# The head of an adaLN block: keys and values by partial sums, modulation rows spread by transfers, a new order of work

## The chip, the cores and the metric

One core of one Trainium2 chip. The metric is the device time of one launch in microseconds (us), here the median of several runs of the same kernel. Engines: PE is TensorE, PEld its weight loads, DVE is VectorE, ACT is ScalarE, POOL is GpSimd, SP is the engine whose queue issues most transfers.

## The reference, cut to what matters

A transformer block with adaptive layer norm: 2048 rows of 512, 32 query heads of 16 that share one head of keys and values, and a dense layer of 1792 with relu.

```python
mod = (_silu(c) @ w_mod).reshape(c.shape[0], 6, 1, -1)
sa, ca, ga, sb, cb, gb = (mod[:, 0], mod[:, 1], mod[:, 2], mod[:, 3], mod[:, 4], mod[:, 5])
h = _layernorm(x, axis=-1) * (1 + ca) + sa
x = x + ga * _A_ref(h, A_wq, A_wk, A_wv, A_wo)     # attention: softmax(q k / sqrt(16)) v, then wo
h = _layernorm(x, axis=-1) * (1 + cb) + sb
x = x + gb * _B_ref(h, B_w1, B_w2)                 # relu(h w1) w2
```

## The kernel before, in words

All engines run an order written out by hand; each engine takes its instructions in that order. The kernel has three stages.

**The head** (up to the first matmul on the values, L1053). The 2048 rows come in four blocks b of 512. A block is loaded (`load_x`), its row sums are taken, it is normalised in place, turned (`tr1`, a transposition of 128 columns at a time through a `ps_exp` bank, then ScalarE writes `hT` with the modulation as scale and bias), and then keys and values (`kv`) and the first six of 16 query projections (`qproj_now`, one at a time in the bank `ps_fill`) are made from it. The first unit of queries needs the maxima of its scores before its exponentials can run: `max_of` makes 48x512 scores in one of four banks (three `ps_max`, one `ps_more`) and VectorE takes their maximum. There are 64 such steps for unit 0, 16 for each 512 keys (`kb`), in the order of `kb`, and 16 for unit 1.

The string `FIRST` is the order of the head after block 0 is turned. Each letter emits one step on all engines that it needs:

- `A`, `B`: the two halves of the first query projection; each ends with a low part on VectorE (L410), which frees its `ps_exp` bank
- `x`, `y`: row statistics of 128 rows of block 1, block 2, on VectorE (L233); `s`: the same for block 3, on ScalarE (L302, L304); `c`, `E`, `f`: the ends of these statistics for blocks 1, 2, 3 (`E` and `f` mostly on GpSimd, begun by three small VectorE instructions); `c`, `r`, `g`: the rows of blocks 1, 2, 3 are normalised, two on GpSimd (L326), two on ScalarE (L329)
- `t`: one transposition step; `q`: a quarter of a query projection (four matmul instructions of 256 columns); after four of them ScalarE copies the bank out and rounds it (L278, L266) and GpSimd makes the low part
- `k`: one step of `kv`; `m`: one maximum; `d`: one block of scores and its exponential; `o`: one step of the modulation rows; `w`: a dummy matmul; `L`, `l`: loads of queries and weights on SP

`kv` before: four matmuls of 128 rows and 512 columns add up in one bank, ScalarE copies values and keys out (L374, L377: keys as rounded `fp32r`), then the rest that rounding left (the low part, 16 rows of `kp` in each half of the partitions) is made on GpSimd (L385), for block 0 on VectorE (L383). The maxima over these keys need the low parts: half 1 first, then half 0. Last step: the values are turned and VectorE copies them out (L391).

`mod_all` before: 16 narrow matmuls (32 output rows, four side by side in the array) give four partial rows for one modulation vector, and a matmul with `firsts` adds them up and spreads them over 128 partitions (L216). It runs for four vectors: two gates (`gr`), `sbr` and `cbr`. The rows for the first layer norm are made earlier by `mod_row` and `mod_col`.

A query tile's row maxima go through DRAM: `max_rows` transposes them, ScalarE and GpSimd split them, SP stores them and loads them back as two rows of the query tile (L494, L500). Only then can `d` run for that unit.

**The main loop**: 256 cycles `c`. A cycle has eight score blocks with exponentials, eight maxima for a later unit, eight narrow matmuls on the values, and a portion of the dense layers or query projections, in halves of 64 rows. Strings such as `PARTS` give the order in a cycle, and `hook` the position in it at which put-off work is emitted (`put_off`: roundings of tiles that a portion has finished).

**The last cycles** (`ending`, from the point where no maxima are left) have 20 positions (`LAST`, `APART`), all before the values. In some of them the put-off work is the relu and rounding of the hidden layer on ScalarE, then VectorE (L733, L734). After that comes the last block alone.

Of the kernel before, what the change touches and what calls it, by code (L numbers as in the profile page):

```python
# [35 lines left out]
FIRST = ("AxxxkkkxykLwqcykyqyqBEmmmmttqkttsrmmmmkklkmmmsmqqstmmmmq"  # L36
         "qstmmmmkfqqtmmmmkktmmgmmkkmmmmtqtqtmmmmkkkmmmmtkmmkmmomm"
         "mmqqmmmmkommommmqmmmommmommqmmmqoqommmmoqdmmdddmmdmqmmdd"
         "md")
# [25 lines left out]
def build(tc, nc, cst, sb, ps, dr, x, wq, wk, wv, wo, w1, w2, c, w_mod, out):  # L65
# [18 lines left out]
    def chunks(ap):  # L84
        return ap.rearrange("(k p) n -> p k n", p=P)
# [31 lines left out]
    wkv0 = sb.tile([P, DC, 2, DH], F32, name="wkv0", tag="stg", bufs=3)  # L117
    nc.sync.dma_start(wkv0[:, :, 0], chunks(wk))
    nc.sync.dma_start(wkv0[:, :, 1], chunks(wv))
    load_x(1)  # L120
    load_wq(1)
# [20 lines left out]
    firsts = cst.tile([P, P], F32, name="firsts")  # L142
    nc.gpsimd.memset(firsts, 0.0)
    for k in range(DC):
        nc.gpsimd.memset(firsts[k * 32:k * 32 + 1], 1.0)
    wkv = sb.tile([P, 512], F32, name="wkv", tag="pvs", bufs=1)
    wkvr = wkv.rearrange("p (k a n) -> p k a n", k=DC, a=8)
# [63 lines left out]
    def mod_all(i, dst, bank):  # L211

        row = mod_row(i, ps_exp())
        yield
        pt = bank()
        nc.tensor.matmul(pt, firsts, row, start=True, stop=True)  # L216
        nc.scalar.activation(dst, pt, AF.Copy, bias=1.0 if i == 4 else 0.0)
        yield
# [143 lines left out]

    def kv(b):

        bs = slice(b * LB, (b + 1) * LB)
        pt = ps_exp()
        for k in range(DC):
            nc.tensor.matmul(pt, wkv[:, k * P:(k + 1) * P], hT[b][:, k],  # L368
                             start=k == 0, stop=k == DC - 1)
            if k < DC - 1:  # L370
                yield
        vT = sb.tile([P, LB], F32, name="vT", tag="tmp", bufs=2)
        if b:
            nc.scalar.activation(vT, pt, AF.Copy)  # L374
        for g in (1, 0):
            r = slice(g * 64, g * 64 + 48)
            nc.scalar.activation(kp[r, bs], pt[r], AF.Copy)  # L377
        if b == 0:
            nc.scalar.activation(vT, pt, AF.Copy)
        for g in (1, 0):  # L380
            r = slice(g * 64 + 32, g * 64 + 48)
            if b == 0:
                nc.vector.tensor_tensor(kp[r, bs], pt[r], kp[r, bs].bitcast(F32), op=OP.subtract)  # L383
            else:
                nc.gpsimd.tensor_tensor(kp[r, bs], vT[r], kp[r, bs].bitcast(F32), op=OP.subtract)  # L385
        yield
        pv = ps_exp()
        for t in range(4):
            nc.tensor.transpose(pv[:, t * 32:(t + 1) * 32], vT[32:64, t * P:(t + 1) * P],
                                idn[32:64, 32:64])  # L390
        nc.vector.tensor_copy(  # L391
            vt[:, b * 4:(b + 1) * 4, 0:DH],
            pv[:, 0:128].rearrange("p (t n) -> p t n", n=32)[:, :, 16:32])
        yield
# [571 lines left out]
    def sums_of(b):  # L966
        for t in range(4):
# [8 lines left out]
                          wqs.rearrange("p k (a d) -> p k d a", d=DH))  # L976
    for j in range(8):
        nc.gpsimd.tensor_copy(wkvr[:, :, j], wkv0[:, :, 1 if j % 4 == 3 else 0])
# [8 lines left out]
    mods = [mod_all(i, dst, ps_exp) for i, dst in  # L987
            ((2, gr[:, 0]), (5, gr[:, 1]), (3, sbr), (4, cbr))]
# [4 lines left out]
                 o=itertools.chain(*mods))  # L993
    early = [(s, ct) for cts in ((1, 3), (0, 2)) for s in range(2) for ct in cts]
    waiting, ready = list(first_max), 0
    for what in FIRST:
        if what == "m":
            assert waiting[0][4] < (ready + 1) // (DC + 1)
# [11 lines left out]
        elif what == "l":  # L1010
            load_q(1)
        elif what == "d":
# [48 lines left out]
    for c in range(NU * KT // 2):  # L1061
# [19 lines left out]
        hook = 9 if parts is QUERIES else 3  # L1081
# [77 lines left out]
```

## Time and profile before

| | |
|---|---|
| median of 3 runs | 1604.93 us (1603.21 to 1607.35) |
| profiled execution | 1607.23 us, of which the span of the engines' work is 1605.3 us |
| busy in the span | PE 99%, PEld 56%, DVE 85%, ACT 75%, POOL 24% |
| granted TensorE clock | 0.999 |
| head | up to 95.2 us |

The profile lists busy time of each engine, groups of instructions by line with their mean duration and the idle time of the engine before them (with what ended it), the chain of work that ended last, and timelines. Times in a row of the timeline are start and duration in us; a bracket at the end gives the idle time before it and the instruction that ended it.

### The profile page before, as it was taken

How to read it: one execution, taken by the hardware profiler on the slowest of the kernel's cores; microseconds unless marked ns; L12 is line 12 of the kernel's file. 1: busy time of each engine (PE TensorE's matmuls, PEld its weight loads, DVE VectorE, ACT ScalarE, POOL GpSimd, SP SyncE). 2: the span in 40 equal slices, each digit the busy share in tenths (PEclk: the TensorE clock that was granted, in tenths of full speed). 3: DMA queues.
4: the chain of work that ended last, by engine and by line, in shares of the span. 5: the costliest groups of instructions: out<-in, count | busy, mean ns of one | idle time of the engine just before them, and what ended most of it. 6: DMA issues, size and time to landing. Idle time of an engine off the chain costs nothing.

```text
span 1605.3 us, 33595 instructions
## 1 busy us (share of the span) xinstructions
PE 1591.2 (99%) x12919; PEld 900.3 (56%) x12919; DVE 1358.4 (85%) x2377; ACT 1207.2 (75%) x2368; POOL 379.6 (24%) x581
## 2 busy tenths in 40 slices
PE   8999999999999999999999999999999999999999
PEld 5545454446655565556655565556655565546668
DVE  6889999998889888998889988898889988898331
ACT  4567888778877887778877787778877788778931
POOL 3323365541113110141112211131112311131010
PEclk9999999999999999999999999999999999999999
DMA  8334543323211330114201331113201331122331
GB/s 268 121 111 132 163 128 94 104 85 99 69 37 51 99 106 17 61 44 128 70 24 48 98 106 32 51 55 116 83 20 47 89 109 42 37 69 93 128 131 54
DMA packets 96486, 137.16 MB, mean 85 GB/s; under 512 B 24328, under 2 KB 59852, under 8 KB 96328
## 3 DMA queue, kind: packets, MB, share of 16 engines
q1 hardware_dynamic: 96048, 134.83, 27.1%
q8 instruction: 103, 1.69, 0.4%
q14 instruction: 55, 0.45, 0.1%
q10 hardware_dynamic: 280, 0.20, 0.0%
HBM read 104.00 MB, written 28.82 MB: 83 GB/s over the span
## 4 chain that ended last, share of the span: by engine, by line
PE 94%; DVE 3%; ACT 1%; DMA 1%; issue 0%; POOL 0%; POOLq 0%; SPq 0%; PEldq 0%; DVEq 0%; ACTq 0%
PE ps_pv L1053 31%; PE ps_exp L909 22%; PE ps_fill L185 19%; PE ps_max L530 16%; DVE pm L532 1%; PE ps_exp L162 1%; PE ps_max L162 1%; PE ps_fill L162 1%; PE ps_exp L368 1%; ACT pe L911 1%; DMA xb<-in_A_x_dram 0%; DMA recs<-rc 0%; PE ps_max L172 0%; PE ps_max L909 0%; PE ps_exp L335 0%
## 5 line engine op out<-in xcount | busy, mean ns | idle before, releaser
L532 DVE TENSOR_REDUCE pm<-ps_max 128x1 f32<-128x512 f32 x2022 | 1258.4, 681 | 142.0 <-PE ps_max L530 122.0
L911 ACT ACTIVATE pe<-ps_exp 128x512 f32<-128x512 f32 x2017 | 1062.9, 605 | 285.0 <-PE ps_fill L185 124.5
L530 PE MATMUL ps_max<-kp,qp 48*128 48x512 f32 x2022 | 836.8, 425 | 0.7 <-DVE pm L532 0.7
L909 PE MATMUL ps_exp<-qp,kp 50*128 50x512 f32 x2017 | 752.6, 414 | 2.3 <-ACT pe L911 2.1
L1053 PE MATMUL ps_pv<-pe,vt 128*32 128x512 f32 x4096 | 543.8, 604 | 0.0
L909 PEld LDWEIGHTS ps_exp<-qp,kp 50*128 50x128 f32 x2017 | 352.0, 185 | 300.7 <-ACT pe L911 182.2
L530 PEld LDWEIGHTS ps_max<-kp,qp 48*128 48x128 f32 x2022 | 369.0, 185 | 211.0 <-DVE pm L532 179.8
L185 PE MATMUL ps_fill<-w2r,r 64*128 64x512 f32 x1008 | 273.2, 403 | 0.0
L185 PE MATMUL ps_fill<-hh,w1s 64*128 64x256 f32 x1472 | 214.5, 286 | 0.1
L185 PEld LDWEIGHTS ps_fill<-hh,w1s 64*128 64x128 f32 x1472 | 193.2, 187 | 0.5 <-PEq L178 0.4
L185 PEld LDWEIGHTS ps_fill<-w2r,r 64*128 64x128 f32 x1008 | 175.1, 184 | 8.0
L1053 PEld LDWEIGHTS ps_pv<-pe,vt 128*32 128x32 f32 x4096 | 82.0, 108 | 129.5 <-issue 111.8
L267 POOL TENSOR_TENSOR r<-stg,r 128x512 fp32r<-128x512 f32 x46 | 59.2, 1286 | 276.0 <-ACT r L266 269.1
L185 PE MATMUL ps_fill<-hl,w1s 64*128 64x256 f32 x736 | 118.3, 280 | 0.0
L185 PEld LDWEIGHTS ps_fill<-hl,w1s 64*128 64x128 f32 x736 | 99.5, 186 | 0.0
L185 PE MATMUL ps_fill<-hT,wq 64*128 64x256 f32 x320 | 81.9, 375 | 0.0
L1116 POOL TENSOR_TENSOR on<-num,den 128x256 f32<-128x256 f32 x31 | 22.8, 737 | 238.6 <-DMA den<-recs 144.8
L185 PEld LDWEIGHTS ps_fill<-hT,wq 64*128 64x128 f32 x320 | 59.4, 186 | 5.5
L925 POOL COPY num<-pvs 128x256 f32<-128x256 f32 x32 | 12.7, 398 | 196.0 <-ACT pvs L921 196.0
L491 POOL TENSOR_TENSOR ms<-sq,ms 128x32 fp32r<-128x32 f32 x28 | 7.1, 255 | 138.8 <-ACT ms L486 138.8
L278 ACT ACTIVATE stg<-ps_fill 128x512 f32<-128x512 f32 x61 | 37.5, 614 | 0.5 <-PE ps_fill L162 0.5
L185 PE MATMUL ps_fill<-wol,oh 64*128 64x512 f32 x112 | 36.6, 407 | 0.0
(194 smaller groups left out, 1020.7 us busy)
## 6 DMA issues: line engine op xcount, KB each, us to landing
w1s<-w1dr SPq DMA_DIRECT2D x104, 512.0 KB
qp<-qdr SPq DMA_DIRECT2D x64, 192.0 KB
qdr<-qq SPq DMA_DIRECT2D x39, 256.0 KB
raw<-in_B_w_dram SPq DMA_DIRECT2D x28, 256.0 KB
w1dr<-w1s SPq DMA_DIRECT2D x14, 512.0 KB
wmod<-in_w_mod_dram SPq DMA_DIRECT2D x6, 1024.0 KB
x<-in_A_x_dram SPq DMA_DIRECT2D x8, 512.0 KB
out_dram<-ot SPq DMA_DIRECT2D x16, 256.0 KB
```

The costliest lines, as they stand in the source:

```text
L162: nc.tensor.matmul(pt[0] if isinstance(pt, tuple) else pt, w, a, start=start, stop=stop is True)
L185: ins = nc.tensor.matmul(pt, w[r], a[r], start=start and h == 1, stop=stop and h == 0)
L267: (eng or nc.gpsimd).tensor_tensor(lo, src, hi.bitcast(F32), op=OP.subtract)
L278: nc.scalar.activation(stg, pt, func, **kw)
L368: nc.tensor.matmul(pt, wkv[:, k * P:(k + 1) * P], hT[b][:, k], start=k == 0, stop=k == DC - 1)
L530: nc.tensor.matmul(pt, qps[u][i][r, j * P:(j + 1) * P], kp[r, kb * 512:(kb + 1) * 512], start=True, stop=True)
L532: nc.vector.tensor_reduce(pms[u][:, (hf * 2 + i) * 4 + j, kb:kb + 1], pt, axis=AX.X, op=OP.max)
L909: nc.tensor.matmul(pt, kp[r, kt * P:(kt + 1) * P], qps[u][ct // 2][r], start=True, stop=True)
L911: nc.scalar.activation(pe, pt, AF.Exp)
L925: nc.gpsimd.tensor_copy(num, pvs[:, 0:TB])
L1053: nc.tensor.matmul(pvt[at:at + 32], vt[:, kt], pes.pop((s, i)), start=(kt == 0), stop=(kt == KT - 1))
L1116: due[1]()
```

## The change

Keys and values: the four matmuls of a block get 32 output rows each and run side by side in four column groups, so a bank holds four partial sums of 32 rows. ScalarE copies it to a tile (`each`), and one matmul with `gather` (ones in the right places, made on GpSimd from the identity) adds the four and spreads keys and values over the partitions as before. `kv` has three steps in place of five. The weights are loaded straight into place. The first keys' low parts go to GpSimd and get a letter of their own, `p`.

Modulation rows: one routine `mods_all` does all four vectors in two steps `o`. Vector n has the column group n, and the four parts of its sum add up in the bank. ScalarE copies the bank out (twice, one with bias 1.0); the rows are stored to DRAM and loaded back to 128 partitions by broadcasting loads on SP.

Order: a new string `FIRST`, without `w`; the load of the second part of `wq` moves ahead of block 1. In the last cycles `hook` is 19 in place of 3: a portion's roundings are emitted behind the scores of the cycle that finished it, not among the scores of the next.

```diff
-FIRST = ("AxxxkkkxykLwqcykyqyqBEmmmmttqkttsrmmmmkklkmmmsmqqstmmmmq"
-         "qstmmmmkfqqtmmmmkktmmgmmkkmmmmtqtqtmmmmkkkmmmmtkmmkmmomm"
-         "mmqqmmmmkommommmqmmmommommqmmmqoqommmmoqdmmdddmmdmqmmdd"
-         "md")
+FIRST = ("xxAxxkqkLcpyyyyEBkqttttmmmmkmmmmksmmmmqkrsmmmmqslmmmmtts"
+         "fmmmmttmmmmkmmmmkqgkmmmmttmmmmttmmmmkqmmmmkqkmmmmqqmmmmq"
+         "qmmmmqqmmmmqqqommmqommmmqqdmmdddmmdqmmddmmd")
...
-    wkv0 = sb.tile([P, DC, 2, DH], F32, name="wkv0", tag="stg", bufs=3)
-    nc.sync.dma_start(wkv0[:, :, 0], chunks(wk))
-    nc.sync.dma_start(wkv0[:, :, 1], chunks(wv))
+    wkv = sb.tile([P, 512], F32, name="wkv", tag="pvs", bufs=1)
+    wkvr = wkv[:, 0:P].rearrange("p (k a n) -> p k a n", k=DC, a=2)
+    nc.sync.dma_start(wkvr[:, :, 0], chunks(wk))
+    nc.sync.dma_start(wkvr[:, :, 1], chunks(wv))
+    load_wq(1)
     load_x(1)
-    load_wq(1)
     load_x(2)
...
-    def mod_all(i, dst, bank):
-
-        row = mod_row(i, ps_exp())
-        yield
-        pt = bank()
-        nc.tensor.matmul(pt, firsts, row, start=True, stop=True)
-        nc.scalar.activation(dst, pt, AF.Copy, bias=1.0 if i == 4 else 0.0)
+    def mods_all(dst):
+
+        pt = ps_exp()
+        rows = sb.tile([P, D], F32, name="mrows", tag="pe", bufs=11)
+        mods = dr.tile([4, D], F32, name="mods")
+        for k in range(DC):
+            for n, i in enumerate(dst):
+                nc.tensor.matmul(pt[n * 32:(n + 1) * 32], sgb[:, k], wm[i][:, k],
+                                 start=k == 0, stop=k == DC - 1)
+            if k == 1:
+                yield
+        nc.scalar.activation(rows[0:96], pt[0:96], AF.Copy)
+        nc.scalar.activation(rows[96:P], pt[96:P], AF.Copy, bias=1.0)
+        for n, to in enumerate(dst.values()):
+            nc.sync.dma_start(mods[n:n + 1], rows[n * 32:n * 32 + 1])
+        for n, to in enumerate(dst.values()):
+            nc.sync.dma_start(to, mods[n:n + 1].to_broadcast([P, D]))
         yield
...
         for k in range(DC):
-            nc.tensor.matmul(pt, wkv[:, k * P:(k + 1) * P], hT[b][:, k],
-                             start=k == 0, stop=k == DC - 1)
-            if k < DC - 1:
-                yield
+            nc.tensor.matmul(pt[k * 32:(k + 1) * 32], wkv[:, k * 32:(k + 1) * 32], hT[b][:, k],
+                             start=True, stop=True)
+        each = sb.tile([P, 512], F32, name="kvk", tag="pe", bufs=11)
+        nc.scalar.activation(each, pt, AF.Copy)
+        yield
+        pt = ps_exp()
+        nc.tensor.matmul(pt, gather, each, start=True, stop=True)
         vT = sb.tile([P, LB], F32, name="vT", tag="tmp", bufs=2)
-        if b:
-            nc.scalar.activation(vT, pt, AF.Copy)
+        nc.scalar.activation(vT, pt, AF.Copy)
         for g in (1, 0):
             r = slice(g * 64, g * 64 + 48)
             nc.scalar.activation(kp[r, bs], pt[r], AF.Copy)
-        if b == 0:
-            nc.scalar.activation(vT, pt, AF.Copy)
-        for g in (1, 0):
-            r = slice(g * 64 + 32, g * 64 + 48)
-            if b == 0:
-                nc.vector.tensor_tensor(kp[r, bs], pt[r], kp[r, bs].bitcast(F32), op=OP.subtract)
-            else:
+
+        def low():
+            for g in (1, 0):
+                r = slice(g * 64 + 32, g * 64 + 48)
                 nc.gpsimd.tensor_tensor(kp[r, bs], vT[r], kp[r, bs].bitcast(F32), op=OP.subtract)
+
+        if b:
+            low()
+        else:
+            first_low.append(low)
         yield
...
+    nc.gpsimd.tensor_tensor(sums4, idn[:, 0:32], idn[:, 32:64], op=OP.add)
+    for k in (2, 3):
+        nc.gpsimd.tensor_tensor(sums4, sums4, idn[:, k * 32:(k + 1) * 32], op=OP.add)
     for j in range(8):
-        nc.gpsimd.tensor_copy(wkvr[:, :, j], wkv0[:, :, 1 if j % 4 == 3 else 0])
+        nc.gpsimd.tensor_copy(gather[:, j * DH:(j + 1) * DH],
+                              sums4[:, DH:] if j % 4 == 3 else sums4[:, 0:DH])
...
+        elif what == "p":
+            first_low.pop()()
...
-        hook = 9 if parts is QUERIES else 3
+        hook = 19 if ending else 9 if parts is QUERIES else 3
```

More of the change, by code (lines that the diff above doesn't have):

```diff
@@ L35 @@
 HEAD_Q = 6
-FIRST = ("AxxxkkkxykLwqcykyqyqBEmmmmttqkttsrmmmmkklkmmmsmqqstmmmmq"
-         "qstmmmmkfqqtmmmmkktmmgmmkkmmmmtqtqtmmmmkkkmmmmtkmmkmmomm"
-         "mmqqmmmmkommommmqmmmommmommqmmmqoqommmmoqdmmdddmmdmqmmdd"
-         "md")
+FIRST = ("xxAxxkqkLcpyyyyEBkqttttmmmmkmmmmksmmmmqkrsmmmmqslmmmmtts"
+         "fmmmmttmmmmkmmmmkqgkmmmmttmmmmttmmmmkqmmmmkqkmmmmqqmmmmq"
+         "qmmmmqqmmmmqqqommmmqommmmqqdmmdddmmdqmmddmmd")
 ET = mybir.EngineType
@@ L141, in build @@
     nc.gpsimd.memset(vt, 1.0)
[L142 to L147, printed above, removed]
+    gather, sums4 = wkv[:, P:2 * P], wkv[:, 2 * P:2 * P + 32]
     def warm(n):
@@ L361, in tr_first @@
         yield
+    first_low = []
     def kv(b):
@@ L986, in build @@
     queries0 = first_queries()
-    mods = [mod_all(i, dst, ps_exp) for i, dst in
-            ((2, gr[:, 0]), (5, gr[:, 1]), (3, sbr), (4, cbr))]
+    mods = mods_all({2: gr[:, 0], 5: gr[:, 1], 3: sbr, 4: cbr})
     steps = dict(A=queries0, B=queries0, x=sums1, y=sums2,
@@ L992, in build @@
                  t=itertools.chain(*trs), k=itertools.chain(*kvs),
-                 o=itertools.chain(*mods))
+                 o=mods)
     early = [(s, ct) for cts in ((1, 3), (0, 2)) for s in range(2) for ct in cts]
@@ L997, in build @@
         if what == "m":
-            assert waiting[0][4] < (ready + 1) // (DC + 1)
+            assert waiting[0][4] < (ready + 1) // 3
             max_of(*waiting.pop(0))
```

## The prediction

> **What bounds the kernel now.** I read the page first, then the chain of work by line and in order of time, then the window of the head by group and by time, last the final cycles.
>
> ```profile
> span 1605.3 us, 33595 instructions
> PE 1591.2 (99%) x12919; PEld 900.3 (56%) x12919; DVE 1358.4 (85%) x2377; ACT 1207.2 (75%) x2368; POOL 379.6 (24%) x581
> ```
>
> TensorE is the bound over the whole span. The change touches only the head (up to the first values matmul at 95.20 us) and the last cycles; what lies between is the same work in the same order, so a gain or loss in the head moves the end by as much. In the head TensorE is one of two bounds. The chain in order of time:
>
> ```profile
> 20.63 3.45 PE ps_exp L368 x8
> ...
> 41.78 0.44 PE ps_exp L335 x4
> ...
> 56.50 0.86 PE ps_fill L162 x4
> ...
> 66.52 0.99 PE ps_exp L206 x8
> ...
> 73.39 7.19 DVE pm L532 x12
> ...
> 83.00 0.86 PE ps_exp L216 x2
> ...
> 88.48 0.42 PE ps_exp L909
> ...
> 95.20 0.99 PE ps_pv L1053 x8
> ```
>
> Each block of keys and values costs 3.45 us of TensorE, a transposition step (t) 0.44, a query step (q) 0.86, a quad of narrow matmuls (both passes) 0.99. Twelve maxima in a row take 7.19, so VectorE needs 0.60 for one and 2.4 for a group of four, whatever TensorE does. VectorE between the first maximum (33.39) and the 64th (80.60), by group:
>
> ```profile
> L532 DVE TENSOR_REDUCE pm<-ps_max 128x1 f32<-128x512 f32 x48 | 30.1, 682 | 5.6 <-PE ps_max L530 5.5
> ...
> L315 DVE TENSOR_SCALAR ve<-mv 128x4 f32<-128x4 f32 x1 | 0.2, 171 | 1.4 <-ACT junk L304 1.4
> ```
>
> It idles 7.0 us in 47.2. TensorE can be no more than four banks ahead of it, so a group of four starts when the first maximum of the group before is done.
>
> **What leaves TensorE.** A block's 3.45 becomes one quad and a gathering matmul: 0.99 + 0.86 = 1.85 (the gather by L216, also 128 rows and 512 columns), four times: 6.4 less. The modulation rows lose four L216 of 0.86: 3.4 less; their 16 narrow matmuls stay at four quads. Together 9.8 us of TensorE. ScalarE loses eight copies for the rows, gains two, and four for the partial sums. VectorE loses the two first subtractions. Whether that shows at the end depends on the waits of the new order, so I walk it through with the durations of before.
>
> **The start.** Rows of the timeline:
>
> ```profile
> 21.09 0.42 DVE L410 SCALAR_TENSOR_TENSOR qq<-ps_exp,qq 128x256 fp32r<-128x256 f32 x1 [1.81 <-ACT qq L409]
> ...
> 22.25 0.66 DVE L233 BATCH_NORM_STATS2 st<-xb 128x6 f32<-128x512 f32 x1
> ...
> 23.04 0.66 DVE L233 BATCH_NORM_STATS2 st<-xb 128x6 f32<-128x512 f32 x1
> ...
> 27.39 0.17 DVE L242 TENSOR_SCALAR ve<-mv 128x4 f32<-128x4 f32 x1
> ...
> 29.77 0.16 DVE L310 TENSOR_TENSOR nmy<-nm,y 128x4 f32<-128x4 f32 x1
> 29.84 1.53 POOL L326 TENSOR_SCALAR xb<-xb,nm,y 128x512 f32<-128x512 f32 x2 [12.79 <-DVE y L256]
> ...
> 29.90 0.73 PE L530 MATMUL ps_max<-kp,qp 48*128 48x512 f32 x3
> ...
> 32.85 0.16 DVE L242 TENSOR_SCALAR ve<-mv 128x4 f32<-128x4 f32 x1
> ...
> 33.39 1.88 DVE L532 TENSOR_REDUCE pm<-ps_max 128x1 f32<-128x512 f32 x3
> ```
>
> Statistics (x, y) come every 0.79, the ends of block 1 (c) take 2.5, those of block 2 (E) 0.55 of VectorE. New order: x, x from 19.3, the query's low part at 21.1 to 21.5, x, x to 23.1, c to 25.7 (it ended at 29.9 before), four y to 28.9, E to 29.5, B's low part to 29.9. GpSimd's rows of block 1 (1.53) then end near 27.2 and the first keys' low parts (2.6, row below) near 29.8. The second transposition of block 1 takes the bank that B's low part frees at 29.9, so three transpositions end at 31.3, and the first maximum is read at 31.85: 1.5 earlier than before. The query loads keep their place behind A's stores on SP, so they land as before (by 29.90, when TensorE ran the first maximum on them).
>
> **First wait, the sums of block 3 (f).** ScalarE rows:
>
> ```profile
> 33.98 0.63 ACT L266 ACTIVATE qq<-stg 128x512 fp32r<-128x512 f32 x1
> 34.61 1.45 ACT L343 ACTIVATE hT<-ps_exp,cols 128x512 f32<-128x512 f32 x2
> 35.95 0.62 ACT L302 ACTIVATE junk<-xb 128x512 f32<-128x512 f32 x1
> ...
> 37.41 1.50 ACT L329 ACTIVATE xb<-xb,nmy,y 128x512 f32<-128x512 f32 x2
> ```
>
> One s is 37.41 - 35.95 = 1.46. From 31.85, five groups and one copy of values take VectorE to 44.2; f stands there. It needs the fourth s. Block 1's gather stands behind the eighth maximum, which needs a bank freed at 34.3, so it ends at 35.6. ScalarE then has in its queue: the block's three copies 1.8, four s 5.85, rows of block 2 1.5, a query's copy and rounding 1.25, two transposed tiles 1.45: 11.85, to 47.5. VectorE waits 3.3 (before: 1.4), and f ends at 48.1.
>
> **Second and third wait, the low parts of blocks 2 and 3.** The same chain of before:
>
> ```profile
> 55.52 0.57 ACT L374 ACTIVATE vT<-ps_exp 128x512 f32<-128x512 f32 x1
> 56.10 1.21 ACT L377 ACTIVATE kp<-ps_exp 48x512 fp32r<-48x512 f32 x2
> 56.84 2.60 POOL L385 TENSOR_TENSOR kp<-vT,kp 16x512 fp32r<-16x512 f32 x2 [1.28 <-ACT kp L377]
> ...
> 59.50 0.19 PEld L530 LDWEIGHTS ps_max<-kp,qp 48*128 48x128 f32 x2 [0.28 <-POOL kp L385]
> 59.58 1.89 DVE L532 TENSOR_REDUCE pm<-ps_max 128x1 f32<-128x512 f32 x3 [1.38 <-PE ps_max L530]
> ```
>
> The first maximum on new keys waits for the first low part, the second for the second, 1.3 later. From a gather's end: 0.6 + 0.6 + 0.1 + 1.3 = 2.6, then 0.5 from matmul to VectorE. Before, a whole block of TensorE work lay in between. Now the order is four maxima, gather, one q, the values' turn, the next four on the new keys. The gather starts 0.3 after VectorE begins the last group, so the new keys' first maximum can be read at 0.3 + 0.9 + 2.6 + 0.5 = 4.3; VectorE has 2.4 + 0.2 of work: a wait of 1.7, and 0.8 more at the second maximum: 2.5, for block 2 and again for block 3. TensorE's relief is covered by this chain and buys nothing there.
>
> From 48.1: three groups to 55.4; wait 2.5; group to 60.4; 0.65 more, since GpSimd normalises block 3's rows behind the low parts (59.6) and the transpositions stand ahead of the group; three groups to 68.3; wait 2.5; group to 73.4 (this is the 52nd).
>
> **TensorE bound again.** 14 of the 20 q stand behind the 48th maximum. A query's first q waits until its bank is copied out:
>
> ```profile
> 80.60 0.22 DVE L476 TENSOR_REDUCE negm<-pm 128x16 f32<-128x64 f32 x1
> ...
> 81.24 0.58 ACT L278 ACTIVATE stg<-ps_fill 128x512 f32<-128x512 f32 x1
> ...
> 81.87 1.13 PE L162 MATMUL ps_fill<-hT,wq 128*128 128x256 f32 x4 [0.60 <-ACT stg L278]
> ...
> 84.62 0.53 SPq L500 DMA_DIRECT2D qp<-mdr  x2
> ```
>
> Three rounds of two q and four maxima, with two such waits of 0.6, bring TensorE to the 64th maximum at 80.3 and VectorE to 82.6 (80.6 before). Behind it: four q 3.5, two halves of the modulation rows 4.1, seven maxima 1.3, two q 1.8, with some 0.3 of hand-overs: first scores at 91.3. The row maxima's round trip took at most 88.48 - 80.60 = 7.9, so it is over by 90.5. From the first scores to the values it was 95.20 - 88.48 = 6.7, now one maximum fewer, 6.5. So the values start at 97.8 against 95.2: **the head loses 2.6**, although TensorE has 9.8 less to do.
>
> **Rest of the head.** The first reader of the spread rows, and windows of 2 us (busy time of PE, PEld, DVE, ACT, POOL, then granted clock, DMA share, GB/s):
>
> ```profile
> L876 POOL TENSOR_TENSOR raw<-raw,gr x4: 1287/1289/1299, 194.4 to 213.0; 128x512 f32<-128x512 f32 x4
> ```
> ```profile
> 8.00:10.00 2.00, 0.68 (x7) 0.49 (x5) 1.58 (x7) 0.00 (x0) 0.00 (x0) 1.00 1.05 407
> ...
> 12.00:14.00 2.00, 2.00 (x13) 1.94 (x10) 0.00 (x0) 1.81 (x3) 1.20 (x2) 0.55 0.97 258
> 14.00:16.00 2.00, 2.00 (x12) 0.32 (x10) 1.11 (x2) 0.19 (x1) 1.40 (x4) 0.60 0.87 302
> ```
>
> Spreading the rows by transfers puts four stores and four broadcast loads on SP behind the second o; there they wait for ScalarE, and the loads for the stores to land. Queued behind them are the last queries' stores and the loop's first weight loads. I price it at nothing: GpSimd reads the rows first at 194 us. Bounds: nothing, and 4.0 if a store and its load (80.60 to 84.62 for the row maxima) delayed the loop's start in full. Loading wq's second part ahead of block 1 puts 0.25 MB in front of x, 0.9 at 302 GB/s. VectorE wants the block at 19.3 and read it before at 21.4 without a wait; nothing, and at worst 0.9. GpSimd's sums and copies for the gather replace copies and memsets of like size, and nobody waits for them before the first gather at 22.5; without that cover, their few tenths.
>
> **The last cycles.**
>
> ```profile
> 1506.93 0.60 ACT L911 ACTIVATE pe<-ps_exp 128x512 f32<-128x512 f32 x1 [0.41 <-PE ps_fill L172]
> ...
> 1507.90 0.63 ACT L953 ACTIVATE r<-stg 128x512 fp32r<-128x512 f32 x1
> ```
>
> In the last cycles ScalarE's exponentials set the pace; it idles 0.41 before a cycle's first one, and in three cycles (f2 of 4 to 6 in the code) a rounding, 0.52 with its hand-over to the next, stands among them. At position 19 the rounding runs in that idle time, behind the exponentials of its own cycle: 0.4 gained three times, **1.2**. Bounds: 0 and 1.6.
>
> **Sum.** +2.6 - 1.2 = +1.4 on the profiled execution (1607.23 with its surroundings, 2.3 above the median shown): 1604.9 + 1.4 = 1606.3, less than 0.3% (4.8 us, about what a measurement here can tell) from no change.
>
> **The clock.** The new order leaves TensorE waiting about 3 us twice (from 26.6 to 29.9 with one transposition in between, and from 45.8 to 48.8). In the windows above it was busy 0.68 of the 2 us from 8 on, and from 12 to 16 the granted clock was 0.55 and 0.60. The Trainium skill, TensorE: Matmul & The Clock Gate, section on the HAM clock gate, puts the fall after an idle window of about 3.4 us that runs freely. By that rule none of these waits need trip it and the sum stays at 1606.3; by the row they can, and then it is up to the 1610.9 of the second rival.
>
> **Rivals.** *Faster, VectorE binds without the waits.* If ScalarE's and GpSimd's chains run ahead of my queues, all waits named (3.3 + 2.5 + 0.65 + 2.5, and 1.7 in the rounds after) go, 10.7: 1606.3 - 10.7 = 1595.6. For it: VectorE's work from first to 64th maximum is only 40, TensorE's falls by 9.8. Against: each wait is built of measured rows of in-order queues. It is faster than 0.3% once 6.2 of the 10.7 are won. Chance 0.27.
> *Slower, the clock falls.* At half clock, three transpositions and a group at the start cost 1.6, the block and gather behind f 1.1, and the two q and the group behind block 3's wait 1.9: 1606.3 + 4.6 = 1610.9. It decides only if it falls all three times (the first two give 1609.0, still within 0.3%). Against: a wait of 2.4 to 3.3 with some matmuls in it is near the edge. Chance 0.17, with loads that come late.
> *The head's relief and its waits cancel, only the tail shows*: 1603.7; part of my forecast's own range, 1601 to 1609, chance 0.56 for all of that.
>
> Range: from half-way into the faster case, 1597.5, to just short of the full clock case, 1610.5. Chances: faster 0.27, same 0.56, slower 0.17.
>
> **What would show it.** In the changed kernel's trace: narrow L368-type matmuls of about 1 us a block; first maximum near 31.9; VectorE idle before f, released by ScalarE's squares, about 3 us; two waits of TensorE on GpSimd's low parts with VectorE idle about 2.5; 64th maximum near 82.6 and first values near 97.8; no rounding between exponentials in the last cycles. Wrong it would be if the idle before f is under 1 us, or if TensorE reaches the new keys' maxima after the low parts are done.

## The result: 10 us slower, and the profile after

The changed kernel takes 1615.28 us (1614.74 to 1618.84), the kernel before 1604.99 us (1603.21 to 1607.35); the ratio is 1.0067, 95% interval 1.0057 to 1.0078. That is above the range given. The profiled execution took 1614.74 us, 7.5 more than the profiled one before, which was itself 2.3 above the median shown ahead of the prediction. First its page, as for the kernel before:

```profile
span 1613.0 us, 33595 instructions
PE 1592.3 (99%) x12917; PEld 900.5 (56%) x12917; DVE 1358.4 (84%) x2375; ACT 1205.9 (75%) x2366; POOL 380.8 (24%) x581
```

TensorE has less to do, yet its busy time is 1.1 us longer. Where the time went is seen from the group of all matmuls on the values (minimum, median and maximum duration, then the start of the first and of the last), the kernel before above, the changed one below:

```profile
L1053 PE MATMUL ps_pv<-pe,vt x4096: 592/593/618, 95.1 to 1538.4; 128*32 128x512 f32 x196
```
```profile
L1069 PE MATMUL ps_pv<-pe,vt x4096: 592/593/617, 105.1 to 1545.9; 128*32 128x512 f32 x196
```

The head ends 10.0 us later. From there to the last values matmul it takes 1440.8 us where it took 1443.3: the late rounding and some smaller things give 2.5 back. So the whole loss lies in the head. VectorE's rows there, with the idle time before each and what ended it:

```profile
29.98 1.89 DVE L543 TENSOR_REDUCE pm<-ps_max 128x1 f32<-128x512 f32 x3 [2.07 <-PE ps_max L541]
45.69 0.17 DVE L320 TENSOR_SCALAR ve<-mv 128x4 f32<-128x4 f32 x1 [3.52 <-ACT junk L309]
...
57.90 0.69 DVE L543 TENSOR_REDUCE pm<-ps_max 128x1 f32<-128x512 f32 x1 [1.80 <-PE ps_max L541]
59.52 1.29 DVE L543 TENSOR_REDUCE pm<-ps_max 128x1 f32<-128x512 f32 x2 [0.93 <-PE ps_max L541]
62.84 1.89 DVE L543 TENSOR_REDUCE pm<-ps_max 128x1 f32<-128x512 f32 x3 [1.43 <-PE ps_max L541]
...
72.96 0.69 DVE L543 TENSOR_REDUCE pm<-ps_max 128x1 f32<-128x512 f32 x1 [1.77 <-PE ps_max L541]
74.28 1.29 DVE L543 TENSOR_REDUCE pm<-ps_max 128x1 f32<-128x512 f32 x2 [0.63 <-PE ps_max L541]
79.51 1.89 DVE L543 TENSOR_REDUCE pm<-ps_max 128x1 f32<-128x512 f32 x3 [3.35 <-PE ps_max L541]
...
89.38 0.22 DVE L487 TENSOR_REDUCE negm<-pm 128x16 f32<-128x64 f32 x1
```

The waits that the prediction named are all there and of about its size: 3.52 before `f`, 1.80 + 0.93 at block 2's keys, 1.77 + 0.63 at block 3's. But the 64th maximum comes 6.8 us after the predicted time, although `f` was 1.9 early. The windows of 2 us tell why (the column after POOL is the granted clock):

```profile
46.00:48.00 2.00, 0.92 (x2) 0.40 (x2) 1.97 (x5) 0.99 (x2) 1.17 (x6) 0.92 0.46 174
48.00:50.00 2.00, 2.00 (x7) 0.77 (x10) 2.00 (x5) 0.00 (x0) 1.39 (x8) 0.50 0.26 78
...
54.00:56.00 2.00, 1.84 (x9) 0.96 (x7) 0.81 (x3) 1.27 (x3) 0.00 (x0) 0.87 0.01 4
56.00:58.00 2.00, 0.50 (x1) 0.18 (x1) 0.20 (x2) 1.92 (x3) 1.88 (x2) 0.98 0.00 0
58.00:60.00 2.00, 1.30 (x4) 0.65 (x4) 1.07 (x2) 0.00 (x0) 1.89 (x3) 0.50 0.00 0
...
64.00:66.00 2.00, 2.00 (x14) 1.40 (x16) 1.84 (x4) 1.51 (x2) 0.00 (x0) 0.81 0.00 0
...
74.00:76.00 2.00, 1.93 (x7) 0.80 (x5) 1.72 (x3) 0.00 (x0) 0.00 (x0) 0.75 0.00 0
76.00:78.00 2.00, 1.32 (x3) 1.14 (x4) 0.17 (x1) 1.23 (x2) 0.58 (x1) 0.50 0.00 0
...
80.00:82.00 2.00, 2.00 (x6) 1.61 (x7) 2.00 (x4) 0.00 (x0) 0.00 (x0) 0.55 0.52 187
```

Read in windows of 0.02 us, the clock is 1 or 0.5, and something between only where it changes, so a mean of 0.92 over 2 us is a fall 0.32 before the window's end. TensorE runs at half clock from 47.7 to 54.5, from 57.9 to 64.8 and from 75.0 to 81.8: three times, 6.8 us each, one behind each of the named waits (a shorter fall stands near 27 to 31). TensorE's timeline in the first of them has a quad of the sums and a gather (of the same trace at full clock, at 17.7 and 19.6 us, these rows show 1.07 and 1.02):

```profile
49.50 1.94 PE L375 MATMUL ps_exp<-hT,wkv 128*32 128x512 f32 x8
...
52.52 2.07 PE L381 MATMUL ps_exp<-kvk,wkv 128*128 128x512 f32 x2
```

They were counted at 0.99 and 0.86 us; TensorE is "busy" with doing the same more slowly.

The store and the broadcast loads of the modulation rows ran at 96.0 to 100.2 and nothing on the path waited for them: the first scores ran at 97.8, and GpSimd read the rows first at 204.6.

### The profile page after: what moved, and what is told of

Same layout as the page of the kernel before. It is cut to its first block, busy times and chain, and to the rows that moved or that the text cites. A ratio compares the mean times of both kernels' runs of the same rounds, so it can differ in the third digit from the quotient of the medians.

```text
span 1613.0 us, 33595 instructions
## 1 busy us (share of the span) xinstructions
PE 1592.3 (99%) x12917; PEld 900.5 (56%) x12917; DVE 1358.4 (84%) x2375; ACT 1205.9 (75%) x2366; POOL 380.8 (24%) x581
## 4 chain that ended last, share of the span: by engine, by line
PE 93%; DVE 1%; DMA 0%; ACT 0%; POOL 0%; issue 0%; POOLq 0%; DVEq 0%; PEldq 0%; ACTq 0%
PE ps_pv L1069 31%; PE ps_exp L920 22%; PE ps_fill L180 20%; PE ps_max L541 15%; PE ps_fill L157 1%; PE ps_exp L157 1%; PE ps_max L157 1%; PE ps_max L167 0%; DVE pm L543 0%; PE ps_max L920 0%; PE ps_fill L167 0%; DMA recs<-rc 0%; PE ps_exp L213 0%; ACT pe L922 0%; DMA den<-recs 0%
```

## The experiments

Theory 1: the order leaves TensorE stretches in which it has little to do, the clock falls there, and the half clock eats the relief and more. Rival: the waits of the new queues are the loss, whatever the clock.

| kernel | median us | ratio to before, 95% | first values, us | clock, profiled run |
|---|---|---|---|---|
| changed, dummies at the waits | 1612.42 | 1.0038, 1.0025 to 1.0050 | 101.6 | 0.997 |
| changed, early rounding | 1616.10 | 1.0067, 1.0053 to 1.0081 | 104.9 | 0.994 |
| before + partial sums | 1611.88 | 1.0044, 1.0032 to 1.0057 | 101.0 | 0.995 |
| before + rows, two steps | 1607.20 | 1.0015, 1.0006 to 1.0023 | 96.7 | 0.996 |
| changed, busy everywhere | 1612.05 | 1.0044, 1.0031 to 1.0057 | 101.0 | 1.000 |
| before + rows, four steps | 1604.51 | 0.9997, 0.9988 to 1.0005 | 89.6 | 0.999 |
| even order | 1606.10 | 1.0014, 1.0004 to 1.0023 | 91.4 | 0.995 |
| before + late rounding | 1603.05 | 0.9989, 0.9981 to 0.9998 | 91.6 | 0.999 |
| even order, even tail | 1605.77 | 1.0002, 0.9991 to 1.0013 | 90.8 | 1.000 |
| the same without dummies | 1605.37 | 0.9998, 0.9987 to 1.0008 | 94.2 | 0.996 |
| before + four steps + late rounding | 1603.26 | 0.9991, 0.9981 to 1.0000 | 95.6 | 0.994 |
| changed, keys earlier | 1609.02 | 1.0022, 1.0013 to 1.0031 | 96.0 | 0.998 |
| changed, keys earlier, dummies | 1608.55 | 1.0021, 1.0013 to 1.0030 | 98.2 | 0.997 |
| changed, keys and sums earlier | 1609.05 | 1.0031, 1.0019 to 1.0044 | 96.8 | 0.997 |
| even order, held by dummies | 1603.71 | 0.9991, 0.9982 to 0.9999 | 91.7 | 1.000 |

The median of the kernel before beside them was 1604.22 for the first four, then 1604.99, 1604.85 and 1604.97. Executions of one kernel differ in clock, so the first values of one profile aren't the median's.

**Dummies at the waits.** A digit in the order stands for so many dummy matmuls.

```diff
-...fmmmmttmmmm...kqgkmmmmtt...kqkmmmmqq...
+...fmmmmtt8mmmm...kqgk5m2mmmtt...kqk5m2mmmqq...
```

> The changed kernel with dummy matmuls (128x128 on the identity, results unused) in TensorE's three long waits of the head: eight behind the transpositions after f, and five and two around the first maximum on the keys of block 2 and of block 3. They fit into idle time and nothing else moves. Theory 1 (the loss is the clock: granted 0.50 in most of 48 to 55, 58 to 65 and 75 to 82 us): the clock stays at 1.00 from 46 to 90, the 64th maximum comes 6 to 9 us earlier and the run is 1606 to 1610, that is 6 to 9 below the changed kernel's 1615. Theory 2 (the loss is the order itself: waits, and queries left to the end): the waits for f and for the low parts are as long as before the dummies, the run stays at 1614 to 1616 whatever the clock does.

1612.42, between the two. The falls at 58 and 75 us are gone and the 64th maximum comes at 85.93, 3.45 earlier, with useless work added; the fall behind `f` stayed, from 48.8 to 55.6. One of the five executions kept its clock at 1.000: 1609.0. A third to a half of theory 1's 6 to 9 us shows; in that one execution the order still loses 4 to 5 us at full clock.

**Early rounding.** `hook` back to 3 in the last cycles.

> The changed kernel with the old place of the rounding in the last cycles (hook 3). If the new place fills ScalarE's idle 0.4 us at the start of three cycles, this run is 1.2 to 1.7 us slower than the changed kernel and the roundings stand among the exponentials again; if the new place bought nothing, the two agree within 0.5 us.

Its row shows where: 1442.3 us from first to last where the changed kernel took 1440.8.

```profile
L1069 PE MATMUL ps_pv<-pe,vt x4096: 592/593/617, 104.9 to 1547.2; 128*32 128x512 f32 x196
```

The medians differ by 0.8, under the 1.2 to 1.7 expected; the profiled spans by 1.3, at its low edge.

**Each of the two reliefs alone, in the old order.** First the partial sums (`kv` in three steps, the two freed `k` left as empty steps), then `mods_all` at the 3rd and the 6th of the old eight `o`.

> The kernel before with one part of the change: keys and values by partial sums, in the old order (the quad at the third of the five old steps, the gather at the fourth; first low parts on VectorE as before). Theory 1 (the parts are sound, the new order's waits and the clock cost): TensorE has 6.4 us less to do in the head, of which 1.5 to 2 go to waiting for the extra copy, so 2 to 5 us faster than before, 1600 to 1603. Rival (the longer chain of copy, gather and low part costs more than the matmuls save): same or slower than before, 1605 or more, with longer idle time of VectorE in front of the maxima.

> The kernel before with one part of the change: modulation rows in two steps, spread by transfers, put at the third and sixth of the eight old steps. If TensorE is the bound in this part of the head, its 3.4 us less show nearly in full: 2 to 4 us faster than before, 1601 to 1603. If the eight transfers hold up what stands behind them on SP, or VectorE binds, 0 to 1 us.

Both came out slower where they were expected faster: 1611.88 and 1607.20. For the sums the rival had allowed for it, and its longer idle time of VectorE is there: 3.92, 3.48 and 3.21 us in front of the maxima at 40.1, 58.9 and 64.6. TensorE waits 1.93 us on the copy of the partial sums, and the clock is half from 35.3 to 42.2 and again from 55.8 to 62.7. The wait begins at 35.3, when the clock falls, so it isn't the cause of that fall; ahead of it stand maxima at VectorE's pace and the quad:

```profile
34.26 1.06 PE L370 MATMUL ps_exp<-hT,wkv 128*32 128x512 f32 x8
37.25 2.07 PE L376 MATMUL ps_exp<-kvk,wkv 128*128 128x512 f32 x2 [1.93 <-ACT kvk L373]
```

The rows alone show the same more plainly, a fall at 79.8 without a wait ahead of it (the clock also fell at 11.6 and at 96.9). Windows, then TensorE's timeline ahead of that fall:

```profile
76.00:78.00 2.00, 1.70 (x4) 0.55 (x3) 2.00 (x4) 0.00 (x0) 0.00 (x0) 1.00 0.00 0
78.00:80.00 2.00, 1.90 (x8) 1.08 (x8) 1.97 (x5) 0.00 (x0) 0.00 (x0) 0.96 0.03 8
80.00:82.00 2.00, 1.55 (x5) 0.95 (x4) 1.97 (x5) 1.34 (x3) 0.35 (x2) 0.50 0.01 2
...
84.00:86.00 2.00, 2.00 (x16) 0.39 (x8) 0.00 (x0) 0.00 (x0) 0.00 (x0) 0.50 0.32 117
```
```profile
75.79 1.69 PE L537 MATMUL ps_max<-kp,qp 48*128 48x512 f32 x3
77.58 0.49 PE L537 MATMUL ps_more<-kp,qp 48*128 48x512 f32 x1
78.18 0.49 PE L537 MATMUL ps_max<-kp,qp 48*128 48x512 f32 x1
78.60 1.13 PE L159 MATMUL ps_fill<-hT,wq 128*128 128x256 f32 x4
```

PE counts as busy 1.70 and 1.90 of 2 us, and VectorE is busy throughout: TensorE makes one maximum each 0.6 us, because VectorE gives a bank back each 0.6. Five maxima in 2.8 us, then one quarter of a projection, and the clock falls. Here the busy column isn't activity. Each of these rows shows about 0.5 us for one maximum, where three back to back take 0.66 on the chain of the kernel before, 0.22 each.

**Busy everywhere.** The dummies as above, three more times three among the first transpositions, and maxima on the keys of blocks 1 and 2 made twice:

```diff
+        for _ in range(2 if u == 0 and kb in (1, 2) else 1):
             nc.tensor.matmul(pt, qps[u][i][r, j * P:(j + 1) * P], ...
```

> The changed kernel with TensorE kept busy wherever the first run with dummies still showed a fall: dummies between the first transpositions of block 1, eight behind f, seven around each wait on low parts, and every maximum of the first unit on the keys of blocks 1 and 2 computed twice into its own bank (32 more matmuls of 0.2 us, results the same). Theory 1, the half clock is what the head lost: granted clock 1.00 in all windows from 26 us to 85 us, 64th maximum near 82, first values at 97 to 99, run 1606 to 1609, although TensorE has some 10 us more to do than in the changed kernel. Rival, the waits of the queues themselves cost the time: first values at 102 or later, run 1612 to 1618.

The clock was 1.00 all the way, as wanted, and the run took 1612.05 with the values at 101.0. So at full clock, with the waits and about 7 us of added matmuls (32 of 0.2), it is no faster than with dummies at the waits alone. The rival's number, but it doesn't clear the clock, since the added work is then itself on the path.

**Four steps of rows.**

```diff
-            if k == 1:
+            if k < DC - 1:
                 yield
```

> The kernel before with the modulation rows alone as in the change, but in four steps of one quad each, at the 1st, 3rd, 5th and 7th place of the old eight, so that the 0.99 us quads stand between groups of maxima all the way. TensorE loses four matmuls of 0.86 us. Theory 1, with the activity spread no window gets thin: clock 1.00 from 76 us on, first values at 92 to 94, run 1601 to 1603.5. Rival, those places are paced by VectorE and the row maxima's round trip, so less TensorE work buys nothing whatever the clock: clock 1.00 and first values at 95 to 96, run 1604 to 1605.5. If the clock falls as in the two-step form (79.9 to 86.7 there): 1606 to 1608.

1604.51, the rival's time: no measurable change, against a loss of 0.15% with two steps. The 64th maximum was reached at full clock, first values at 89.6, sooner than either theory had them, but the clock fell at 89.7, where TensorE again made maxima at VectorE's pace, and the loop began at half clock.

**Even order.** The changed code; sums of block 3 ahead of the first maxima, keys made a whole group ahead of their maxima, projections spread over the groups, dummies among the first transpositions.

```diff
-"...EBkqttttmmmmkmmmmksmmmmqkrsmmmmqslmmmmttsfmmmmttmmmmkmmmmkqgk..."
+"...EBkqt3t3st3tsmmmmkrmmmmksmmmmttksmmmmqqlmmmmttfmmmmkgqmmmmkqmmmmktt..."
```

> The changed kernel with another order of the head: two of block 3's sums before the first maxima, f after the fifth group, keys of block 2 and 3 made at least one whole group of maxima before they are read, projections spread one or two to a group, and nine dummies among the first transpositions. Every group of maxima of 2.4 us has 1.7 to 3 us of TensorE work. Theory 1 (thin groups lose the clock, and no wait in it is needed): clock 1.00 from 32 us on, no wait of VectorE over 1 us between the first and the 48th maximum, 64th maximum at 73 to 77, first values at 88 to 92, run 1597 to 1602. Rival, the queues of ScalarE and GpSimd bind the head wherever its steps stand: first values at 97 or later, run 1606 or more.

9 us less than the changed kernel: 64th maximum at 78.24 (89.38), no fall up to 86. From 86.6 to 96.8 the clock was half all the same, behind maxima of the second unit at VectorE's pace, so the median is 1606.10, the rival's number and not the 1602 of theory 1, though the first values at 91.4 are theory 1's.

**Late rounding alone**, on the kernel before.

> The kernel before with the rounding at position 19 in the last cycles, and nothing else of the change. By the trace of the changed kernel (48.32 us from 1490.65 became 46.65) it takes 1.2 to 1.7 us off: 1602.5 to 1603.7. Rival, that stretch was shorter for another reason (the order in which the head left the transfers): within 0.4 us of the kernel before.

1603.05, 1.9 less: as expected, and more than its predicted 1.2. Its head is the code of the kernel before, yet its row reads

```profile
L1053 PE MATMUL ps_pv<-pe,vt x4096: 592/593/1057, 91.6 to 1534.2; 128*32 128x512 f32 x196
```

so the same head took 91.6 here and 95.1 in the profile that the prediction was made from. Where that one lost its 3.5 us is seen at the first modulation matmul, before above, late rounding below:

```profile
8.27 0.69 DVE L233 BATCH_NORM_STATS2 st<-xb 128x6 f32<-128x512 f32 x1 [1.17 <-DMA xb<-in_A_x_dram]
11.07 1.06 PE L206 MATMUL ps_max<-wmod,sgb 128*32 128x512 f32 x8 [2.39 <-DVE y L256]
```
```profile
7.01 0.66 DVE L233 BATCH_NORM_STATS2 st<-xb 128x6 f32<-128x512 f32 x1
9.09 1.07 PE L206 MATMUL ps_max<-wmod,sgb 128*32 128x512 f32 x8
30.05 1.88 DVE L532 TENSOR_REDUCE pm<-ps_max 128x1 f32<-128x512 f32 x3
```

At 11.07 against 9.09 it was 1.98 behind, in a stretch in which VectorE waited 1.17 for a load of rows; only then did the clock fall, from 12.2 to 15.6. At the first maximum (33.39 against 30.05) it was 3.34 behind, so about 1.4 is that fall. Most executions of the kernel before show a mean clock of 1.000 (84 of 105, median 1604.63), the rest 0.999 (1606.28): the profiled one was one of the rest.

**Even tail, with and without dummies.** Projections moved among the last maxima (two of them taken from groups ahead of the lines shown); then the same without the nine dummies.

```diff
-"...mmmmqqmmmm" "qqommmmommmmdmmdddmmdmmddmmd"
+"...mmmmqqmmmm" "mmqommqommmmdqmmddmmqdmmddmmdd"
```

> The even order again, with its end changed: six projections that stood before the 64th maximum or right behind it are spread so that two stand behind the first maxima of the second unit, two beside the halves of the modulation rows and the scores (two fewer ahead), where the clock fell at 86.7 in the first form. Theory 1 (thin stretches lose the clock): granted clock 1.00 from 32 to 95 us, first values at 87 to 90, run 1600 to 1602.5. Rival, VectorE's sixteen maxima and the row maxima's round trip set that end whatever the clock: first values at 91 or later, run 1604 to 1606.5.

> The same order without the nine dummies among the first transpositions. Theory 1: the clock falls once near 27.6 as in the changed kernel's trace, a window or two of 3.4 us, 1 to 3 us more than with dummies. Rival, the start is set by the loads and by VectorE: the same time within 0.7 us.

The profiled execution of the first kept its clock, had the values at 90.8 and took 1602.22; the median is 1605.77, at a clock of 0.998 and in the rival's range. Without dummies three of twelve executions took 1600.3 to 1602.6 at 0.999, the others up to 1608.9 at 0.992 to 0.998. Whether the clock holds differs from one execution to the next; the dummies at the start made no difference, as the rival had it.

**Four steps and late rounding on the kernel before.**

> The kernel before with the rows in four steps and the late rounding. If both effects are real and independent, their measured changes add: -0.5 and -1.9 make 1602.0 to 1603.2. Rival, the two medians differ from the kernel before only by which executions lost the clock: 1604 or more.

1603.26, just above the range expected for the sum of the two (1602.0 to 1603.2), and no less than the late rounding took alone (1603.05): that the four steps add anything isn't shown. The profiled execution lost its clock twice, from 71.5 to 85.2 and from 95.4 to 98.8.

**Keys earlier.** Nothing but this:

```diff
-...fmmmmttmmmmkmmmmkqgkmmmmttmmmmttmmmmkqmmmmkqkmmmmqq...
+...fmmmmttkmmmmkmmmmqgkmmmmttmmmmttkmmmmkqmmmmqkmmmmqq...
```

> The changed kernel with the keys of blocks 2 and 3 made one group of maxima earlier (first step right behind the last transpositions), and nothing else: the two waits on the low parts go, the groups stay as thin as they were. Theory 1 (the clock takes most): both waits of VectorE under 0.6 us, yet the granted clock still falls between 46 and 82 us for at least two windows of 3.4 us, and the run gains only 1 to 4 us, 1611 to 1614.5. Rival (the waits are the loss): the run gains the 5 us of the waits or more, 1608 to 1610.5.

1609.02, 6.3 less, by four letters moved. Its trace, VectorE, then the windows:

```profile
45.17 0.17 DVE L318 TENSOR_SCALAR ve<-mv 128x4 f32<-128x4 f32 x1 [3.56 <-ACT junk L307]
...
54.45 1.29 DVE L541 TENSOR_REDUCE pm<-ps_max 128x1 f32<-128x512 f32 x2 [0.64 <-PE ps_max L539]
57.11 1.89 DVE L541 TENSOR_REDUCE pm<-ps_max 128x1 f32<-128x512 f32 x3 [0.77 <-PE ps_max L539]
61.78 1.89 DVE L541 TENSOR_REDUCE pm<-ps_max 128x1 f32<-128x512 f32 x3 [2.19 <-PE ps_max L539]
```
```profile
56.00:58.00 2.00, 2.00 (x12) 1.17 (x11) 1.23 (x3) 1.45 (x2) 0.00 (x0) 0.68 0.00 0
58.00:60.00 2.00, 2.00 (x10) 1.27 (x11) 1.60 (x3) 1.33 (x2) 0.00 (x0) 0.50 0.00 0
60.00:62.00 2.00, 1.98 (x12) 0.43 (x6) 0.22 (x1) 0.82 (x2) 0.00 (x0) 0.97 0.00 0
```

The wait at block 2's keys fell from 2.7 to 0.64, the one at block 3's from 2.40 to nothing, and of the four falls only one is left, 56.7 to 60.1. The time is the rival's (1608 to 1610.5), but wait and clock went together, so the run doesn't tell them apart: theory 1 had expected two windows or more, the rival no gain from the clock. The wait before `f` is as long as in the changed kernel (3.56) and no fall follows it here.

**Keys earlier, and dummies; keys and sums earlier.** The first adds 3 + 3 + 3 dummies at the start and 8 behind the transpositions that follow `f`, which TensorE runs while VectorE waits; the second moves two `s` to the transpositions of block 1.

```diff
-...Bkqttttmmmm...mmmmttsfmmmmttk...
+...Bkqt3t3t3tmmmm...mmmmttsfmmmmtt8k...
```
```diff
-...Bkqttttmmmmkmmmmksmmmmqkrsmmmmqslmmmmttsfmmmm...
+...Bkqttsttsmmmmkmmmmksmmmmqkrsmmmmqlmmmmttfmmmm...
```

> The changed kernel with the keys of blocks 2 and 3 a group earlier, and dummies between the first transpositions and eight behind the transpositions that stand ahead of f's wait; the wait before f stays at 3.5 us. Theory 1 (what is left over the kernel before is half clock): granted clock 0.999 or more in most executions, 1604.5 to 1606.5, so 2.5 us or more under the run without dummies. Rival (what is left is the wait before f and the order): within 1 us of it, 1608 to 1610.

> The changed kernel with the keys of blocks 2 and 3 a group earlier and two of block 3's sums moved ahead of the first maxima, where ScalarE stood idle 29.9 to 35.3 us but for 1.8 us of copies; no dummies. VectorE's wait before f of 3.5 us should fall under 0.6. Theory 1: that wait was also a thin stretch, so the gain is the wait and a window of half clock, 4 to 5.5 us: 1603.5 to 1605. Rival (TensorE's total is the bound there and the wait is covered): within 1.5 us of the run with earlier keys alone, 1607.5 to 1610.

Both missed theory 1's numbers and are the rival's, 1608.55 and 1609.05. The dummies didn't hold the clock (half at 57.4 to 60.8, 71.0 to 74.5 and 98.4 to 101.8), so that run tells nothing apart. With the sums earlier the wait before `f` is gone, but the transpositions stand behind the two sums on ScalarE, the first of which itself waited until 29.86 for block 3's load, and a wait of 2.25 comes at the start (the 2.06 ahead of it is in the changed kernel too, 2.07):

```profile
29.59 1.89 DVE L541 TENSOR_REDUCE pm<-ps_max 128x1 f32<-128x512 f32 x3 [2.06 <-PE ps_max L539]
34.33 1.89 DVE L541 TENSOR_REDUCE pm<-ps_max 128x1 f32<-128x512 f32 x3 [2.25 <-PE ps_max L539]
```

**Even order, held.**

```diff
-..."mmmmttfm"... "mmqommqommmmdqmmddmmqdmmddmmdd"
+..."mmmmttf4m"... "mmqommqommmm2dqmm1ddmm1qdmm1ddmm1dd"
```

> The even order with the even tail and eleven more dummies: four behind f, two ahead of the first scores, one behind each pair of the second unit's maxima from there on. Theory 1: executions at a clock of 0.999 and more become the rule, median 1600.5 to 1602.5. Rival (the dummies' own time and the loads decide): 1603.5 to 1606 as without them.

1603.71, under both kernels: 0.9991 (0.9982 to 0.9999) of the one before, yet the rival's number and not theory 1's 1600.5 to 1602.5. All eleven executions have a clock of 0.998 or more (even tail alone: down to 0.992). The kernel before with nothing but the late rounding is as fast in the median, and the first values come at 91.7 against 91.6, so that the new head buys anything over the old one is not shown. The executions at a clock of 1.000 hint at it: three of this kernel at 1601.1 to 1601.6, nine of the late rounding alone at 1601.8 to 1604.4.

```profile
L1069 PE MATMUL ps_pv<-pe,vt x4096: 592/593/617, 91.7 to 1532.2; 128*32 128x512 f32 x196
```

**What the clock costs.** Executions of one kernel differ in nothing but what happens on the chip, so they can be set against their mean clock. Mean clock and time of the changed kernel's six, and of the one with keys and sums earlier:

```
0.994 1615.29   0.993 1614.74, 1615.06, 1615.26   0.992 1616.51   0.989 1618.84
0.997 1606.29, 1606.69, 1607.46, 1607.99   0.996 1607.72   0.993 1610.11, 1611.10   0.992 1612.71, 1612.88   0.989 1617.00
```

Within the sixteen kernels (150 executions, one common slope, each kernel with a mean of its own) 0.001 of mean clock goes with 1.1 us; the changed kernel's own six give 0.8. So its 0.993 is worth about 7 x 0.8 to 1.1, 5.8 to 7.5 us of the 10.3. The one execution with dummies at 1.000 lies 6.3 below the changed kernel's median. This is a correlation: an execution in which something came late loses clock and time at once. That clock and loss go together, and that TensorE work without use takes 2.9 us off the median (2.1 against the kernel before beside each), is shown; the split over the whole head is an estimate. For the last of the three falls there is a direct price. From the 52nd maximum to the 64th the changed order is the same in seven of the profiles. It takes 13.2 us where the clock is half for two periods (the changed kernel, and with early rounding), 11.9 where it is half for one (keys earlier with dummies, 71.0 to 74.5) and 10.6 in the four that keep the clock: 2.6 and 1.3 us.

## Why the prediction was wrong

**Right.** The path through the head: the wait before `f` 3.52 (3.3), the waits at the new keys 2.73 and 2.40 (2.5 each), both behind the low parts; the transfers of the rows off the path; the late rounding a gain (1.9 on the kernel before, 1.2 predicted); and that TensorE's 9.8 us less work doesn't come out at the end.

**The step that failed: the clock.** "By that rule none of these waits need trip it and the sum stays at 1606.3" was followed, and the slower rival, which needed three falls, got 0.17. All three places that it named lost the clock (the start, behind `f`, behind block 3's wait), and block 2's wait as well. Its price was small too: 4.6 assumed that only the first steps behind a wait run at half clock, but the three falls behind `f` lasted two periods of 3.41 us each. Two falls fewer, with dummies, moved the 64th maximum by 3.45, so about 1.7 each and 5.2 for three, the last of which alone is 2.6; with the one at the start (0.5: `f` begins at 45.69, and at 45.17 with keys earlier, whose start kept its clock) about 6. The Trainium skill, TensorE: Matmul & The Clock Gate, section on the HAM clock gate, has the window of 3.4 us, and the trace agrees: 47.7 to 54.5 is 6.8, twice 3.41. What was taken from it, that only an idle window trips the clock, is not what these runs show: a window with work for under half of it was enough (last section). The Trainium skill, the same page, section on a second HAM failure mode, psum-queue depth-cycling, tells of a kernel whose clock oscillates because TensorE idles briefly and often between groups; the rows-alone kernel's fall at 79.8, among maxima of 0.22 us made every 0.6, agrees with that. The section gives no price; the prices here are those of the runs.

**The base.** The prediction put +1.4 on the median. It was worked out against a profile whose head had itself lost 3.5 us (95.1 against 91.6), some 2 at a late start and 1.4 in the fall at 12 to 16 us, in 1607.23 us. The row of that fall was quoted, for another purpose. In the changed kernel the start didn't lose it, and `f` ended 1.9 earlier than walked (46.2 against 48.1): corrected for both, the walk gives first values at 95.9 against 91.6, 4.3 and not 2.6. The 1.5 that the new start was to gain at the first maximum is not there: 29.98 against 30.05. The 91.6 is one profile's; starts of the old order vary with the loads (first maximum at 30.05 to 31.38 in four profiles without a fall at the start).

**Smaller terms.** The hand-over ahead of block 3's transpositions, 0.65, measured 1.43 at half clock. At full clock the changed order still took about 1609, 4 us over the kernel before; the walk accounts for some 2.4 of that (4.3 - 1.9). The rest is in the stage called "TensorE bound again". With keys earlier, from the 52nd maximum on the same order at full clock:

```profile
68.93 0.68 DVE L541 TENSOR_REDUCE pm<-ps_more 128x1 f32<-128x512 f32 x1
71.32 1.89 DVE L541 TENSOR_REDUCE pm<-ps_max 128x1 f32<-128x512 f32 x3 [1.71 <-PE ps_max L539]
77.76 1.89 DVE L541 TENSOR_REDUCE pm<-ps_max 128x1 f32<-128x512 f32 x3 [1.36 <-PE ps_max L539]
80.28 0.22 DVE L485 TENSOR_REDUCE negm<-pm 128x16 f32<-128x64 f32 x1
```

The 52nd maximum ends at 69.6, the 64th at 80.2: 10.6, where the walk had 9.2 (73.4 to 82.6). From there to the first values it is 15.7 (to 96.0) where the walk had 15.2. Together 1.9 too little, and 2.4 + 1.9 = 4.3 is about what is seen at full clock. Between `f` and the 52nd maximum the changed kernel took 30.0 for 25.3 walked, with the first two falls in it; with dummies and doubled maxima at full clock it was 28.2, so how much of the 4.7 is the clock stays open beyond 1.8.

**The faster rival** failed as argued: the waits didn't go. Four letters moved took most of the second and third waits away.

## What to carry to other kernels

When TensorE gets less work in a stretch that another engine paces, price the clock first: add up for each 3.4 us there what its matmuls cost back to back, not the busy share, and keep the work that can be moved (projections, transpositions) for the thin groups. See whether the profile that you work from lost clock or came late itself, and compare its own time with the median before you add to either. A producer chain over two engines wants a whole group of other work between its start and its reader, here one place earlier for four letters was worth 6 us.

## What the runs showed of the hardware

The clock fell although TensorE's rows, whose ends the profile models, leave no gap over 0.11 us, when for some 3 us it did one 512-column matmul each 0.6 us (rows alone, 79.8), and came back after one to four periods of 3.41 us: 56.7 to 60.1 in one run, 57.9 to 64.8 in another, 71.5 to 85.2 in a third. Falls of one trace lie on one grid (27.2, 47.7, 57.9 and 75.0 in the changed kernel are 6, 3 and 5 times 3.41 apart), so the same thin stretch can lose the clock in one execution and keep it in the next. The wait before `f` shows it: 3.52 us and a fall in the changed kernel, where TensorE was busy 0.61 us of the period from 44.3 to 47.7, and 3.56 us and no fall with keys earlier, where it was busy 2.32 of the one from 43.1 to 46.5. A kernel near the edge spreads: 1600.3 to 1608.9 for one, at 0.999 to 0.992.

How thin is too thin is an estimate from all seventeen profiles, between 8 and 118 us, by taking each period of the grid at full clock and counting every matmul at what it costs back to back on the chain of the kernel before (a maximum 0.22 us, a transposition instruction 0.11, one of a projection 0.215, one of a gather 0.43, a narrow one of 512 columns 0.43 with up to four side by side). Of 19 periods with work for less than 0.45 of their time 17 were followed by half clock; of 103 with 0.45 to 0.65 it was 12, and of 398 with more none. Neither the busy share of the rows (up to 0.93 ahead of a fall) nor the count of matmuls (2 to 17 begun ahead of a fall, as few as 6 without one) tells them apart.
